# Linear attention with a gated feed-forward: batch 0's k and v in 96 partitions, Newton steps in PSUM, half exchanges as reductions, a new order

## The chip, the cores and the metric

The kernel runs on one core of a Trainium2 chip. The metric is the device time of one execution in microseconds. The core has a matrix engine (TensorE, PE in the profile, with its weight loads as PEld), VectorE (DVE), ScalarE (ACT), GpSimd (POOL) and SyncE (SP), which here issues every DMA. Each engine works through its own queue in order; engines wait for each other by semaphores.

## The reference

Two stages follow each other. Attention is linear, over 8 batches, 8 heads, 576 positions and 64 dimensions:

```python
q_s = exp(q - max(q, axis=-1));  q_s = q_s / (sum(q_s, axis=-1) + 1e-9)
k_s = exp(k - max(k, axis=2));   k_s = k_s / (sum(k_s, axis=2) + 1e-9)
kv  = einsum('bhsd,bhse->bhde', k_s, v)
out = einsum('bhsd,bhde->bhse', q_s, kv)
```

Its 4608 x 512 result x goes through a gated feed-forward with d_ff = 1536:

```python
xn = x / sqrt(mean(x * x, axis=-1) + 1e-6) * rms_g
g = xn @ w_gate;  val = xn @ w_val
return (g * sigmoid(g) * val) @ w_out
```

The weights arrive as 64-bit floats and are converted to 32 bits on the chip.

## The kernel before, in words

**Tiling.** Tokens are taken in 9 blocks (j) of 512, and d_ff in 12 chunks (i) of 128, so that the feed-forward has 108 steps s = 12 j + i. A step is `f1.s.0` and `f1.s.1` (gate and value products, L825, twelve matmuls each), `g_mul`, `silu`, `h_mul`, and `f2.s` (output product, L861). To keep 32-bit accuracy each operand is split into a high and a low part, and three products are summed: `w_hi` and `w_lo` split the gate and value weights, `o_hi` and `o_lo` the output weights, `h_hi` and `h_lo` the activations, `x_hi` and `x_lo` the input. `f2.0` to `f2.8` use plain 32-bit matmuls instead.

**Attention.** Batches b go by pairs of heads (g = 0 to 3). For k: `k_load`, `k_max` over a partition's positions (L445), `k_tr` and `k_top` (maximum over partitions), `k_diag` and `k_rows` (spread of the maximum to all rows), `k_sub` (L471), `k_exp`, then `k_mm` (L484) with v, whose extra column of ones yields the sum. 576 positions lie in 116 partitions of 5: 115 full ones and a last row that holds one position, loaded by a DMA of its own (for k, that position in all five places). In batch 0, v has no column of ones, and `k_mm` multiplies by `ones` in matmuls of their own (L490). Tiles of batch 0 for which no buffers are left lie in weight tiles not yet in use (`scratch`). From block 2 on q is held as 32 x 32 squares, with half of a head's dimensions in each group of 32 partitions, so that maxima and sums are exchanged between halves by `other_half` (L630), called by `q_half` and `q_half2`.

**Normalization.** `n_sum` sums squares by a matmul of mean weights into PSUM, `n_t` transposes, `n_y0` and `n_y1` compute 1/sqrt by a shift, a guess and three Newton steps on tiles of 128 x 16 in SBUF (L748 to L767), `n_rows` and `n_cols` spread the result. `g_mul` needs `n_rows` of its block.

**Weights.** `load_w.i.a` loads (a: gate, value, output); `conv_mul`, `conv_low`, `conv_shift`, `conv_sign` and `conv_add` turn 64 into 32 bits on ACT, DVE and POOL. All of it falls into block 0's time.

**Order.** A list of step names (`ORDER`) fixes the order in which instructions are issued, and so each engine's and SP's queue. A suffix `:A`, `:D` or `:P` puts a step on ACT, DVE or POOL. `warm` issues filler matmuls whose results nobody reads. PSUM has 8 banks: 2 for `ps_gv` (gate, value and `warm`), 4 for `ps_o`, 2 for `ps_a` (attention and `n_sum`). A tile pool hands out its buffers in turn, and the next user of a buffer waits for the last reader.

## Time and profile before

| | |
|---|---|
| median of 3 runs | 1056.67 us (1056.58 to 1057.47) |
| the profiled execution | 1055.17 us |
| its span, first to last instruction | 1053.4 us |
| mean granted TensorE clock | 0.986 |
| DMA | 57.62 MB, mean 55 GB/s |

A view of the profile gives busy time by engine; in the view by stage each row has start and end of the stage, its length, then for PE, PEld, DVE, ACT and POOL the busy time with the count of instructions, then the granted clock, the share of the 16 DMA engines that was busy, and GB/s. A row of a group has line, engine, operation, tiles (out<-in) and shapes, count, then busy us and mean ns, then the engine's idle time ahead of it and what ended it. A row of the timeline has start and duration, and in brackets the idle time ahead. Rows of waits give the waiting and the awaited instruction, total us, count and the longest.

### The profile page before, as it was taken

How to read it: one execution, taken by the hardware profiler on the slowest of the kernel's cores; microseconds unless marked ns; L12 is line 12 of the kernel's file. 1: busy time of each engine (PE TensorE's matmuls, PEld its weight loads, DVE VectorE, ACT ScalarE, POOL GpSimd, SP SyncE). 2: the span in 40 equal slices, each digit the busy share in tenths (PEclk: the TensorE clock that was granted, in tenths of full speed). 3: DMA queues.
4: the chain of work that ended last, by engine and by line, in shares of the span. 5: the costliest groups of instructions: out<-in, count | busy, mean ns of one | idle time of the engine just before them, and what ended most of it. 6: DMA issues, size and time to landing. Idle time of an engine off the chain costs nothing.

```text
span 1053.4 us, 14281 instructions
## 1 busy us (share of the span) xinstructions
PE 1015.6 (96%) x4972; PEld 809.4 (77%) x4972; DVE 603.8 (57%) x1180; ACT 573.6 (54%) x795; POOL 723.6 (69%) x623
## 2 busy tenths in 40 slices
...
GB/s 151 263 192 174 139 115 23 83 33 27 45 46 38 40 41 42 45 33 41 25 74 33 33 34 63 43 33 34 52 41 19 6 40 1 1 1 41 0 1 40
DMA packets 124884, 57.62 MB, mean 55 GB/s; under 512 B 95924, under 2 KB 118796, under 8 KB 124812
## 3 DMA queue, kind: packets, MB, share of 16 engines
...
q8 instruction: 39, 0.64, 0.3%
q14 instruction: 33, 0.27, 0.1%
...
## 4 chain that ended last, share of the span: by engine, by line
PE 59%; DVE 15%; DMA 12%; issue 4%; POOL 4%; ACT 4%; SPq 2%; ACTq 0%; DVEq 0%; POOLq 0%
PE ps_gv L825 35%; PE ps_o L861 20%; DMA kt<-in_k_dram 8%; DVE sw L630 4%; PE ps_a L688 2%; DVE cm L445 2%; DVE ke L471 1%; DVE gs L837 1%; SPq L558 1%; DVE w L382 1%; DMA raw<-in_moe_w_out_dram 1%; DVE kv_lo L532 1%; DVE gs L830 1%; DMA w<-in_k_dram 1%; POOL wl L802 1%
## 5 line engine op out<-in xcount | busy, mean ns | idle before, releaser
L802 POOL TENSOR_TENSOR wl<-w,wh 128x512 fp32r<-128x512 f32 x216 | 281.3, 1308 | 91.5 <-ACT wh L327 87.3
L825 PE MATMUL ps_gv<-xh,wh 128*128 128x512 f32 x864 | 244.0, 403 | 9.4 <-DVE gs L830 7.7
L825 PE MATMUL ps_gv<-xl,wh 128*128 128x512 f32 x864 | 233.8, 391 | 0.0
L825 PE MATMUL ps_gv<-xh,wl 128*128 128x512 f32 x864 | 233.5, 391 | 0.0
L825 PEld LDWEIGHTS ps_gv<-xh,wh 128*128 128x128 f32 x864 | 157.5, 189 | 44.4 <-issue 9.4
L825 PEld LDWEIGHTS ps_gv<-xl,wh 128*128 128x128 f32 x864 | 162.7, 188 | 35.6
L825 PEld LDWEIGHTS ps_gv<-xh,wl 128*128 128x128 f32 x864 | 162.7, 188 | 35.2
L846 POOL TENSOR_TENSOR hl<-gs,hh 128x512 fp32r<-128x512 f32 x99 | 128.2, 1295 | 67.7 <-ACT hh L327 64.8
L834 ACT ACTIVATE gs<-gs 128x512 f32<-128x512 f32 x108 | 68.2, 632 | 193.7 <-DVE gs L830 193.2
L830 DVE TENSOR_TENSOR gs<-ps_gv,r 128x512 f32<-128x512 f32 x108 | 74.4, 689 | 153.1 <-PE ps_gv L825 119.0
L810 POOL TENSOR_TENSOR ol<-w,oh 128x512 fp32r<-128x512 f32 x99 | 128.0, 1293 | 4.5 <-ACT oh L327 4.1
L837 DVE TENSOR_TENSOR gs<-ps_gv,gs 128x512 f32<-128x512 f32 x108 | 74.4, 689 | 95.8 <-PE ps_gv L825 76.5
L327 ACT CAST wh<-w 128x1024 fp32r<-128x1024 f32 x102 | 106.6, 1045 | 35.7 <-PE ps_gv L825 27.3
L861 PE MATMUL ps_o<-oh,hh 128*128 128x512 f32 x396 | 107.4, 393 | 0.0
L861 PE MATMUL ps_o<-ol,hh 128*128 128x512 f32 x396 | 106.9, 392 | 0.0
L861 PE MATMUL ps_o<-oh,hl 128*128 128x512 f32 x396 | 106.7, 392 | 0.0
L327 ACT CAST oh<-w 128x512 fp32r<-128x512 f32 x99 | 61.2, 618 | 62.6 <-PE ps_o L861 61.7
L327 ACT CAST hh<-gs 128x512 fp32r<-128x512 f32 x97 | 60.1, 619 | 64.0 <-DVE gs L837 61.1
L861 PEld LDWEIGHTS ps_o<-oh,hl 128*128 128x128 f32 x396 | 74.9, 189 | 15.8
L861 PEld LDWEIGHTS ps_o<-ol,hh 128*128 128x128 f32 x396 | 74.8, 189 | 16.0
L861 PEld LDWEIGHTS ps_o<-oh,hh 128*128 128x128 f32 x396 | 73.4, 188 | 14.9
L445 DVE TENSOR_REDUCE cm<-kt 116x128 f32<-116x640 f32 x30 | 39.0, 1301 | 62.4 <-DMA kt<-in_k_dram 62.3
...
## 6 DMA issues: line engine op xcount, KB each, us to landing
...
```

The source lines that it names most:

```text
L327: (e.copy if e is nc.scalar else e.tensor_copy)(dst, src)
L445: nc.vector.tensor_reduce(out=cm, in_=kt_[b, g].rearrange("p h j d -> p h d j"), axis=AX.X, op=ALU.max)
L630: nc.vector.tensor_copy(sw[32 * (a ^ 1):32 * (a ^ 1) + 32], st[32 * a:32 * a + 32])
L688: nc.tensor.matmul(px[:, c0:c1], lhsT=wt, rhs=mv[:, c0:c1], start=(i == 0), stop=(i == 2))
L802: on(nc.gpsimd).tensor_tensor(out=wl[:, a], in0=W(s % NF, a), in1=wh[:, a].bitcast(F32), op=ALU.subtract)
L810: on(nc.vector).tensor_tensor(out=ol, in0=W(s % NF, 2), in1=wo_[s][0].bitcast(F32), op=ALU.subtract)
L825: nc.tensor.matmul(pd[s], lhsT=m[:, a, c * P:(c + 1) * P], rhs=X[j, c][x], start=(n == 1), stop=(n == 3 * NKT))
L830: nc.vector.tensor_tensor(out=gs, in0=g_[s], in1=r_[s // NF], op=ALU.mult)
L834: nc.scalar.activation(g_[s], g_[s], AF.Silu)
L837: nc.vector.tensor_tensor(out=g_[s], in0=v_[s], in1=g_[s], op=ALU.mult)
L846: on(nc.gpsimd).tensor_tensor(out=hl, in0=g_[s], in1=h_[s][0].bitcast(F32), op=ALU.subtract)
L861: nc.tensor.matmul(po[t], lhsT=a[:, t * P:(t + 1) * P], rhs=w, start=(i == 0 and n == 0), stop=(i == NF - 1 and n == len(terms) - 1))
```

## The change

Batch 0's positions lie in 96 partitions of 6 (`C0`, `P0`), which leaves no last row, so that each k load is one DMA and each v load one per head; v gets its column of ones by `v_ones`, and `k_mm` is 12 matmuls without those by `ones`. The tiles of all four pairs lie in weight tiles. `k_max0` takes batch 0's maximum in three `tensor_tensor` steps. `k_sub` and `k_exp` of every batch write over k's own tile, and the tile `ke` is gone. `k_diag` may run on ACT, and does in all but one place. `other_half` and `n_cols` copy by a `tensor_reduce` over an axis of length one. The Newton steps keep `ms` and `u` in the PSUM bank that `n_sum` wrote, and each step multiplies in another sequence. In the last step, `f2` goes by token tile and then by term. Of `ORDER`, all lines are new; parts of it are shown. The first `warm` is 16 matmuls instead of 28; the other 20 calls of `warm`, two matmuls each, all stand ahead of `f1.1.0`, where before five of them stood between steps 9 and 10 and one later.

```diff
-constants k_load.0.0 q_load0.0.0 kv_zero0.0 warm.28 kv_zero0.1 k_load.0.1 kv_zero.4 kv_zero.5 kv_zero.6 k_load.0.2
...
-k_rows.0.0 k_max.0.2 warm.2.5 warm.2.1 v_load.0.3 k_sub.0.0 k_tr.0.2 warm.2.10 g_load q_max0.0.1 k_exp.0.0 load_w.0.0
-q_sum0.0.0 q_sub0.0.1:P load_w.1.0 k_top.0.1 load_w.2.0 k_max.0.3 load_w.3.0 q_exp.0.1 k_mm.0.0 k_load.1.0 k_diag.0.1
-q_max0.0.2 k_rows.0.1 load_w.0.1 k_tr.0.3 q_eps0.0.0 warm.2.2 k_top.0.2 q_sub0.0.2:P load_w.0.2 q_rec0.0.0 warm.2.6
-k_sub.0.1 load_w.1.1 warm.2.15 load_w.1.2 q_mul0.0.0:P q_exp.0.2 q_max0.0.3 q_load0.1.0 k_exp.0.1 q_sum0.0.1
...
-conv_low.0.2.1 w_lo.0.1:P warm.2.12 q_max0.1.0 conv_mul.2.0.2:A f1.0.0.0 k_top.1.0 conv_add.1.0.2:P f1.0.1.0
-conv_low.2.0.2 f1.0.0.1 conv_mul.1.2.1:A f1.0.1.1 conv_low.1.2.1 n_y0.0 f1.0.0.2 w_hi.1.0.2:A f1.0.1.2
-conv_shift.0.2.1 f1.0.0.3 conv_mul.3.0.2:A n_y1.0 f1.0.1.3 conv_low.3.0.2 w_lo.1.0:P n_rows.0 k_max.1.1
-conv_mul.2.2.1:A w_lo.1.1:P conv_low.2.2.1 g_mul.0 q_sub0.1.0:P conv_mul.3.2.1:A q_max0.1.1 conv_low.3.2.1 f1.1.0
...
-n_hi.5:A g_mul.59 n_lo.5:P silu.59 n_sum.5 h_mul.59 w_hi.61.0.2:A f2.58 n_t.5 h_hi.59:A w_lo.61.0:P q_max.7.0
...
+constants k_load.0.0 q_load0.0.0 v_ones.0.0 warm.16 k_load.0.1 v_ones.0.1 kv_zero0.0 q_load0.0.1 v_ones.0.2 v_ones.0.3
+kv_zero0.1 k_load.0.2 kv_zero.4 q_load0.0.2 kv_zero.5 kv_zero.6 kv_zero.7 v_load.0.0 kv_zero.0 kv_zero.1 k_load.0.3
+kv_zero.2 q_load0.0.3 kv_zero.3 v_load.0.1 k_max0.0.0 v_load.0.2 q_max0.0.0 k_tr.0.0 warm.2.0 v_load.0.3 k_top.0.0
+q_sub0.0.0:P k_diag.0.0:A k_rows.0.0 g_load k_sub.0.0 warm.2.1 q_exp.0.0 load_w.0.0 load_w.1.0 k_max0.0.1 k_load.1.0
+q_max0.0.1 k_tr.0.1 k_exp.0.0 warm.2.5 load_w.2.0 q_sum0.0.0 q_sub0.0.1:P load_w.3.0 k_top.0.1 k_load.1.1 k_mm.0.0
+q_max0.0.2 k_diag.0.1:A q_exp.0.1 k_max0.0.2 k_rows.0.1 warm.2.2 q_eps0.0.0 warm.2.6 k_max0.0.3 load_w.0.1 k_tr.0.2
+warm.2.10 load_w.0.2 q_rec0.0.0 q_sub0.0.2:P k_top.0.2 k_tr.0.3 warm.2.15 k_sub.0.1 k_diag.0.2:A k_rows.0.2
+q_mul0.0.0:P load_w.1.1 q_exp.0.2 warm.2.11 q_max0.0.3 load_w.1.2 k_exp.0.1 q_sum0.0.1 q_sub0.0.3:P q_t0.0.0
+q_load0.1.0 k_top.0.3 k_sub.0.2 k_diag.0.3:A q_exp.0.3 warm.2.3 k_eps.0.0 k_rows.0.3 q_c0.0.0:A q_eps0.0.1 k_mm.0.1
...
+k_tr.1.0 warm.2.8 conv_shift.0.2.1 conv_mul.1.0.2:A warm.2.12 w_lo.0.0:P n_y0.0 warm.2.13 k_top.1.0 warm.2.17
+conv_low.1.0.2 n_y1.0 warm.2.9 w_lo.0.1:P f1.0.0.0 conv_low.0.2.1 warm.2.18 k_diag.1.0:A conv_shift.1.0.2
+conv_mul.1.2.1:A f1.0.0.1 n_rows.0 conv_mul.2.0.2:A f1.0.1.0 conv_sign.1.0.2 f1.0.0.2 conv_low.2.0.2 f1.0.1.1
+conv_sign.0.2.1 conv_low.1.2.1 f1.0.0.3 conv_add.1.0.2:D conv_mul.2.2.1:A f1.0.1.2 conv_low.2.2.1 g_mul.0
+conv_add.0.2.1:P k_rows.1.0 w_hi.1.0.2:A f1.0.1.3 q_max0.1.0 warm.2.14 conv_shift.2.0.2 silu.0 load_w.4.0 warm.2.19
+w_lo.1.0:P k_sub.1.0 load_w.4.1 f1.1.0 load_w.4.2 q_max0.1.1 w_lo.1.1:P k_exp.1.0 n_cols.0 h_mul.0 q_sub0.1.0:P
...
+w_hi.59.0.2:A q_t.6.1 q_sum.6.3 h_lo.57:P f1.58.0 n_hi.5:A q_half2.6.3 o_hi.58:A w_lo.59.0:P q_load.7.0 n_lo.5:P
+f1.58.1 g_mul.58 silu.58 w_lo.59.1:P o_lo.58:P f2.57 h_mul.58 w_hi.60.0.2:A q_sum2.6.3 q_rec.6.3 h_hi.58:A w_lo.60.0:P
+q_max.7.0 h_lo.58:P f1.59.0 q_half.7.0 o_hi.59:A w_lo.60.1:P o_lo.59:P f1.59.1 g_mul.59 q_mul.6.3:P silu.59 q_max2.7.0
+q_sub.7.0:P n_sum.5 h_mul.59 w_hi.61.0.2:A f2.58 n_t.5 h_hi.59:A w_lo.61.0:P n_y0.5 q_hi.6.0:A q_hi.6.1:A n_y1.5
...
     SF = FULL * CH
+    C0 = 6
+    P0 = S // C0
+
+    def scratch0(wi, g):
+        return scratch(wi, g * 2 * C0 * D, [P0, 2, C0, D])
 
...
         hs = slice(2 * g, 2 * g + 2)
-        if b == 0 and g >= 2:
-            kt = scratch(3, (g - 2) * 640, [KP, 2, CH, D]).rearrange("p (h j d) -> p h j d", h=2, j=CH)
-        else:
-            kt = ap.tile([KP, 2, CH, D], F32, name="kt")
+        if b == 0:
+            kt_[b, g] = scratch0(3, g).rearrange("p (h j d) -> p h j d", h=2, j=C0)
+            nc.sync.dma_start(kt_[b, g], k[b, hs].rearrange("h (p j) d -> p h j d", j=C0))
+            return
+        kt = ap.tile([KP, 2, CH, D], F32, name="kt")
         nc.sync.dma_start(kt[:FULL], k[b, hs, :SF].rearrange("h (p j) d -> p h j d", j=CH))
...
         if (b, g) not in vt_:
-            if b == 0 and g >= 2:
-                vt_[b, g] = scratch(2, (g - 2) * 650, [KP, 2, CH, D]).rearrange("p (h j d) -> p j h d", j=CH, h=2)
-            elif b == 0:
-                vt = ap.tile([KP, CH, 2, D + 1], F32, name="vt").rearrange("p j h d -> p (j h d)")
-                vt_[b, g] = vt[:, :2 * CH * D].rearrange("p (h j d) -> p j h d", j=CH, h=2)
+            if b == 0:
+                n = 2 * C0 * (D + 1)
+                vt = scratch(2, g * n, [P0, n]) if g < 3 else scratch(1, 0, [P0, n])
+                vt_[b, g] = vt.rearrange("p (j h d) -> p j h d", j=C0, h=2)
             else:
...
         if b == 0:
-            nc.sync.dma_start(vt[:FULL].rearrange("p j h d -> p h j d"),
-                              v[b, hs, :SF].rearrange("h (p j) d -> p h j d", j=CH))
-        else:
             for h in range(2):
-                nc.sync.dma_start(
-                    vt[:FULL, :, h, :D],
-                    v[b, 2 * g + h, :SF].rearrange("(p j) d -> p j d", j=CH))
+                nc.sync.dma_start(vt[:, :, h, :D], v[b, 2 * g + h].rearrange("(p j) d -> p j d", j=C0))
+            return
+        for h in range(2):
+            nc.sync.dma_start(
+                vt[:FULL, :, h, :D],
+                v[b, 2 * g + h, :SF].rearrange("(p j) d -> p j d", j=CH))
         nc.sync.dma_start(
...
     def k_max(b, g):
-        cm = ap.tile([P, P], F32, name="cm")[:KP].rearrange("p (h d) -> p h d", h=2)
+        cm = ap.tile([P, P], F32, name="cm")[:KP if b else P0].rearrange("p (h d) -> p h d", h=2)
         nc.vector.tensor_reduce(out=cm, in_=kt_[b, g].rearrange("p h j d -> p h d j"), axis=AX.X, op=ALU.max)
...
 
+    def k_max0(b, g):
+        e = nc.vector
+        kt = kt_[b, g]
+        m = scratch(1, 2 * C0 * (D + 1) + g * C0 * D, [P0, 2, C0 // 2, D]).rearrange("p (h j d) -> p h j d", h=2, j=C0 // 2)
+        cm = cm_[b, g] = ap.tile([P, P], F32, name="cm")[:P0].rearrange("p (h d) -> p h d", h=2)
+        e.tensor_tensor(out=m, in0=kt[:, :, :C0 // 2], in1=kt[:, :, C0 // 2:], op=ALU.max)
+        e.tensor_tensor(out=m[:, :, 0], in0=m[:, :, 0], in1=m[:, :, 1], op=ALU.max)
+        e.tensor_tensor(out=cm, in0=m[:, :, 0], in1=m[:, :, 2], op=ALU.max)
+
     def k_tr(b, g):
         kps[b, g] = attn_ps(b == 0)
-        nc.tensor.transpose(out=kps[b, g][:, :KP], in_=cm_[b, g].rearrange("p h d -> p (h d)"),
-                            identity=ident[:KP, :KP])
+        n = KP if b else P0
+        nc.tensor.transpose(out=kps[b, g][:, :n], in_=cm_[b, g].rearrange("p h d -> p (h d)"),
+                            identity=ident[:n, :n])
 
...
         kx_[b, g] = small.tile([P, 1], F32, name="kx")
-        nc.vector.tensor_reduce(out=kx_[b, g], in_=kps[b, g][:, :KP], axis=AX.X, op=ALU.max)
+        nc.vector.tensor_reduce(out=kx_[b, g], in_=kps[b, g][:, :KP if b else P0], axis=AX.X, op=ALU.max)
 
...
         kd_[b, g] = ap.tile([P, P], F32, name="cm")
-        on(nc.vector).tensor_scalar_mul(kd_[b, g], ident, kx_[b, g])
+        scaled(kd_[b, g], ident, kx_[b, g], nc.vector)
 
     def k_rows(b, g):
-        mb = kps[b, g][:KP, P:2 * P]
-        nc.tensor.matmul(mb, lhsT=ones[:, :KP], rhs=kd_[b, g], start=True, stop=True)
+        n = KP if b else P0
+        mb = kps[b, g][:n, P:2 * P]
+        nc.tensor.matmul(mb, lhsT=ones[:, :n], rhs=kd_[b, g], start=True, stop=True)
         mb_[b, g] = mb.rearrange("p (h d) -> p h d", h=2)
...
     def k_sub(b, g):
-        if b == 0 and g >= 2:
-            ke = scratch(2, 1300 + (g - 2) * 640, [KP, CH, 2, D]).rearrange("p (j h d) -> p j h d", h=2, j=CH)
-        else:
-            ke = ap.tile([KP, CH, 2, D], F32, name="ke")
-        on(nc.vector).tensor_tensor(out=ke.rearrange("p j h d -> p h j d"), in0=kt_[b, g],
-                                in1=mb_[b, g].unsqueeze(2).broadcast_to([KP, 2, CH, D]), op=ALU.subtract)
-        ke_[b, g] = ke
+        n, c = (KP, CH) if b else (P0, C0)
+        ke = ke_[b, g] = kt_[b, g]
+        on(nc.vector).tensor_tensor(out=ke, in0=ke, in1=mb_[b, g].unsqueeze(2).broadcast_to([n, 2, c, D]),
+                                    op=ALU.subtract)
 
...
         ps = attn_ps(b == 0)
-        for j in range(CH):
-            n = KP if j == 0 else FULL
+        rows = [KP] + [FULL] * (CH - 1) if b else [P0] * C0
+        for j, n in enumerate(rows):
             for h in range(2):
-                nc.tensor.matmul(ps[h * D:(h + 1) * D, :D + (b > 0)], lhsT=ke[:n, j, h], rhs=vt[:n, j, h],
-                                 start=(j == 0), stop=(j == CH - 1))
-        if b == 0:
-            for j in range(CH):
-                n = KP if j == 0 else FULL
-                for h in range(2):
-                    nc.tensor.matmul(ps[h * D:(h + 1) * D, D:D + 1], lhsT=ke[:n, j, h], rhs=ones[:n, :1],
-                                     start=(j == 0), stop=(j == CH - 1))
+                nc.tensor.matmul(ps[h * D:(h + 1) * D, :D + 1], lhsT=ke[:n, h, j], rhs=vt[:n, j, h],
+                                 start=(j == 0), stop=(j == len(rows) - 1))
         kps[b, g] = ps
...
     def q_load0(j, g):
-        if j == 0 and g >= 2:
-            qt = scratch(3, 1280 + (g - 2) * TB, [P, TB])
+        if j == 0 and g == 3:
+            qt = ap.tile([P, TB], F32, name="r")
         else:
...
         for a in range(4):
-            nc.vector.tensor_copy(sw[32 * (a ^ 1):32 * (a ^ 1) + 32], st[32 * a:32 * a + 32])
+            nc.vector.tensor_reduce(out=sw[32 * (a ^ 1):32 * (a ^ 1) + 32], in_=st[32 * a:32 * a + 32].unsqueeze(2),
+                                    axis=AX.X, op=ALU.max)
         return sw
...
         if j == 0 and g < 3:
-            sq = fp.tile([P, TB], F32, name="gs", bufs=3) if g else scratch(3, 1280 + 2 * TB, [P, TB])
+            sq = fp.tile([P, TB], F32, name="gs", bufs=3)
         elif j and g == 0:
...
 
-    def n_eps(j):
-        ms_[j] = small.tile([P, M], F32, name="ms", bufs=1)
+    def n_y0(j):
+        ps = ms_[j]
+        ms_[j], u_[j] = ps[:, :M], ps[:, M:2 * M]
+        n_y[j] = small.tile([P, M], F32, name="y", bufs=2)
         nc.vector.tensor_scalar_add(ms_[j], dg_[j][:, :, 0], EPS_RMS)
-
-    def n_half(j):
-        u_[j] = small.tile([P, M], F32, name="u", bufs=1)
         nc.vector.tensor_scalar(out=u_[j].bitcast(I32), in0=ms_[j].bitcast(I32), scalar1=1, scalar2=None,
                                 op0=ALU.logical_shift_right)
-
-    def n_guess(j):
-        n_y[j] = small.tile([P, M], F32, name="y", bufs=2)
         nc.vector.tensor_scalar(out=n_y[j].bitcast(I32), in0=u_[j].bitcast(I32), scalar1=-1.0,
...
 
-    def n_newton(j, k):
+    def n_y1(j):
         y, u = n_y[j], u_[j]
-        if k % 3 == 0:
-            nc.vector.tensor_tensor(out=u, in0=y, in1=y, op=ALU.mult)
-        elif k % 3 == 1:
-            nc.vector.scalar_tensor_tensor(out=u, in0=u, scalar=-0.5, in1=ms_[j], op0=ALU.mult, op1=ALU.mult)
-        else:
+        for _ in range(3):
+            nc.vector.scalar_tensor_tensor(out=u, in0=y, scalar=-0.5, in1=ms_[j], op0=ALU.mult, op1=ALU.mult)
+            nc.vector.tensor_tensor(out=u, in0=u, in1=y, op=ALU.mult)
             nc.vector.scalar_tensor_tensor(out=y, in0=u, scalar=1.5, in1=y, op0=ALU.add, op1=ALU.mult)
...
             p = slice(32 * a, 32 * a + 32)
-            nc.vector.tensor_copy(yt[p], n_y[j][p].rearrange("p (t a) -> p a t", a=4)[:, a])
+            nc.vector.tensor_reduce(out=yt[p], in_=n_y[j][p].rearrange("p (t a) -> p a t", a=4)[:, a].unsqueeze(2),
+                                    axis=AX.X, op=ALU.max)
         y_[j] = yt
-
-    def n_y0(j):
-        for f in (n_eps, n_half, n_guess):
-            f(j)
-        for k in range(3):
-            n_newton(j, k)
-
-    def n_y1(j):
-        for k in range(3, 9):
-            n_newton(j, k)
 
...
             terms = ((hh, oh), (hh, ol), (hl, oh))
-        for n, (a, w) in enumerate(terms):
-            for t in range(T):
+        order = [(n, t) for n in range(len(terms)) for t in range(T)]
+        if s == NS - 1:
+            order.sort(key=lambda x: (x[1], x[0]))
+        for n, t in order:
+                a, w = terms[n]
                 nc.tensor.matmul(po[t], lhsT=a[:, t * P:(t + 1) * P], rhs=w, start=(i == 0 and n == 0),
```

480 lines of the change are left out of this document (236 added, 244 removed).

## The prediction

> **What bounds the kernel now.** I read the busy shares first, then the view of busy time by stage, then the timelines of the stages in which TensorE is not at its pace. All times are of the profiled execution.
>
> ```profile
> PE 1015.6 (96%) x4972; PEld 809.4 (77%) x4972; DVE 603.8 (57%) x1180; ACT 573.6 (54%) x795; POOL 723.6 (69%) x623
> ```
>
> TensorE is the engine to follow, but its 96% contains filler matmuls (`warm`), and a head in which no matmul of the feed-forward can start. By stage, cut at the first gate matmul (47.12), at later chunks' and blocks' starts and at the last matmul's end:
>
> ```profile
> core 0: us, PE busy (x) PEld busy (x) DVE busy (x) ACT busy (x) POOL busy (x), PEclk, DMA share, GB/s
> 47.12:58.20 11.08, 5.67 (x25) 4.35 (x25) 10.70 (x19) 9.74 (x13) 6.92 (x6) 0.96 0.37 113
> 58.20:66.50 8.30, 8.30 (x24) 6.62 (x25) 5.65 (x9) 4.44 (x6) 2.69 (x2) 0.64 0.68 184
> 66.50:141.50 75.00, 73.05 (x321) 48.57 (x320) 68.06 (x99) 54.39 (x70) 52.88 (x38) 1.00 0.62 183
> 141.50:175.74 34.24, 33.26 (x149) 23.59 (x150) 26.72 (x33) 21.61 (x32) 29.70 (x24) 1.00 0.15 37
> 175.74:294.23 118.49, 109.09 (x542) 87.77 (x540) 79.51 (x177) 65.52 (x90) 86.31 (x75) 0.99 0.19 43
> 294.23:848.00 553.77, 547.56 (x2772) 445.19 (x2773) 338.05 (x709) 316.53 (x435) 402.34 (x342) 1.00 0.16 39
> 848.00:1048.10 200.10, 200.07 (x883) 165.28 (x881) 49.73 (x86) 77.98 (x113) 125.08 (x100) 1.00 0.03 11
> ```
>
> A stage's length less its PE time is PE's idle time: 5.4, 0, 2.0, 1.0, 9.4, 6.2 and nothing, 24.0 in all. From 294 on, where most of the time lies, only 6.2 us can be had, and the matmuls of these stages stay as they are. What is left to gain lies in the 47.12 us ahead of the first gate matmul, in its wait, in the half clock behind it (8.30 at 0.64 loses about 3.0) and in the stages up to 294.
>
> What holds the head is the loading:
>
> ```profile
> 12.00:14.00 2.00, 1.89 (x9) 1.32 (x10) 1.78 (x3) 0.00 (x0) 0.00 (x0) 1.00 0.33 120
> 34.00:48.00 14.00, 14.00 (x61) 8.56 (x60) 8.64 (x16) 11.67 (x21) 6.46 (x7) 0.78 0.96 299
> 56.00:58.00 2.00, 0.00 (x0) 0.00 (x0) 2.00 (x4) 1.07 (x1) 0.00 (x0) 0.82 0.38 86
> 5.00:47.12 42.12, 35.24 (x255) 25.33 (x254) 24.93 (x54) 21.73 (x38) 13.41 (x13) 0.80 0.76 229
> 18.19 0.27 SPq L429 DMA_DIRECT2D w<-in_v_dram  x1
> 38.84 0.67 ACT L332 ACTIVATE w<-raw 128x512 f32<-128x512 f32 x1 [0.21 <-DMA raw<-in_moe_w_val_dram]
> 47.12 0.39 PE L825 MATMUL ps_gv<-xh,wh 128*128 128x512 f32 x1
> 58.20 2.04 PE L825 MATMUL ps_gv<-xh,wh 128*128 128x512 f32 x4 [5.41 <-DVE gs L830]
> ```
>
> From 12 to 14, where k and v in 115 partitions are what is under way, the DMA share is 0.33: 5.3 of 16 engines, 120 GB/s. Weights, in 128 partitions, get 0.96 and 299 GB/s. The last v of batch 0 is issued at 18.19 and the weights queue behind it; ACT begins on chunk 0's value weights only as they land, at 38.84, and 8.3 us later the first gate matmul runs.
>
> **Part 1, the loads: -8.9 us.** Batch 0's k and v are 8 x 0.295 = 2.36 MB, at 120 GB/s 19.7 us. What 96 partitions get is not in this trace. Lower bound: no more engines, and v, now in pieces of 64 elements as later batches' v is, at the 86 GB/s of 56 to 58, where such v is loading: 9.8 + 13.7 = 23.5, 3.8 longer. Upper bound: all engines, 16/5 of these rates but no more than the weights' 299: k 3.9, v at 275 GB/s 4.3, so 8.2, 11.5 shorter. I take 11.3, near the upper end, because the nearest row of a partition count that divides evenly is the 128-partition one. Eight transfers of k's and v's last row go, four issues come (v by head). Against it, `k_load.1.1` (0.29 MB in 115 partitions, 2.4 us) now stands ahead of `load_w.0.1`: 11.3 - 2.4 = 8.9. ACT's step moves to 30, the first gate matmul to 38. DVE's work must keep up: 24.93 us from 5 on, which ends by 30 if never idle, so 38 leaves 8 us for latencies. The other head edits cost or save little there:
>
> ```profile
> L445 DVE TENSOR_REDUCE cm<-kt 116x128 f32<-116x640 f32 x30 | 39.0, 1301 | 62.4 <-DMA kt<-in_k_dram 62.3
> L830 DVE TENSOR_TENSOR gs<-ps_gv,r 128x512 f32<-128x512 f32 x108 | 74.4, 689 | 153.1 <-PE ps_gv L825 119.0 <-PE ps_a L450 23.8 <-POOL wl L802 4.8
> L637 DVE TENSOR_TENSOR st<-st,sw 128x16 f32<-128x16 f32 x28 | 4.7, 169 | 0.6
> 7.79 1.04 POOL L582 TENSOR_TENSOR qt<-qt,st 128x512 f32<-128x512 f32 x1 [2.92 <-DVE st L578]
> ```
>
> By L637 and L830 an element costs DVE 1.05 ns over a fixed 0.15: `k_max0`'s 384, 128 and 128 elements take 1.1 us against 1.30. The 20 matmuls with `ones` go from a PE that waits there. Should POOL's passes (1.04 each) hold `k_max0`'s three instructions, up to 3 us come onto the first pair: 1031, to which I give 10%, inside the forecast's span.
>
> The Trainium skill, "DMA: Bandwidth & Descriptors", section "Why a DMA increments its semaphore by 16 and not by 1", says that a transfer runs on the largest number of engines up to 16 that divides its slowest dimension. By it 115 rows get 5 and 96 rows 16; the 5.3 above agree for 115, and no run here shows 96. "SBUF — State Buffer", section "Who interferes with whom", of the Trainium skill says that a DVE instruction with two SBUF inputs is held by a GpSimd instruction that reads SBUF, and a reduction never: that speaks against `k_max0`, and would be the 1031.
>
> **Part 2, Newton in PSUM: -3.5 us, and -2 of the half clock.**
>
> ```profile
> 47.57 0.50 DVE L748 TENSOR_SCALAR ms<-sq 128x16 f32<-128x16 f32 x1
> 48.00 2.45 POOL L387 TENSOR_TENSOR w<-w,raw 128x1024 int32<-128x1024 int32 x1
> 48.10 2.38 DVE L752 TENSOR_SCALAR u<-ms 128x16 int32<-128x16 int32 x1
> 55.63 0.71 DVE L771 STREAM_TRANSPOSE r<-y 128x512 f32<-128x512 f32 x1
> L763 DVE TENSOR_TENSOR u<-y 128x16 f32<-128x16 f32 x27 | 12.5, 463 | 0.9
> ```
>
> A shift of 16 elements takes 2.38 us and ends with POOL's addition, which began 0.1 us before it: DVE was held, not working. The mean of 463 ns against 169 (L637) for the same shape says that this is common. The twelve steps and one conversion (0.4) fill 47.57 to 55.63; at 0.2 a step they take 2.4 instead of 7.6, 5.2 saved. The new order puts more conversion ahead of `g_mul.0` (two `conv_sign` and a `conv_add` on DVE, against one `k_max`), which takes back some 1.7. The wait of 5.41 falls to about 2; of the 3.0 lost to the clock I take 2, as `warm.2.14` and `warm.2.19` now fill the gap. Should PSUM operands be held too, both terms are nothing; all steps at 0.17 and no conversion ahead would give 5.4 and 3.0.
>
> **Part 3, half exchanges, `k_diag`, order up to 294: -11 us.**
>
> ```profile
> L630 DVE COPY sw<-st 32x16 f32<-32x16 f32 x112 | 50.3, 449 | 2.0
> L630 DVE COPY sw<-sm 32x16 f32<-32x16 f32 x112 | 40.2, 359 | 2.0
> L455 DVE TENSOR_REDUCE kx<-ps_a 128x1 f32<-128x116 f32 x28 | 7.5, 270 | 8.1 <-PE ps_a L450 8.1
> L459 DVE TENSOR_SCALAR cm<-ident,kx 128x128 f32<-128x128 f32 x32 | 19.3, 604 | 0.7
> L327 ACT CAST kv_hi<-ot 128x128 fp32r<-128x128 f32 x4 | 1.2, 296 | 0.0
> 153.01 3.89 PE L392 MATMUL ps_gv<-mean_w 128*128 128x512 f32 x10 [0.54 <-DVE gs L830]
> 236.30 0.45 PE L688 MATMUL ps_a<-qh,kv_hi 128*128 128x384 f32 x1 [2.94 <-DVE kv_hi L334]
> 237.54 4.33 PE ps_o L861 x12
> 247.36 2.72 PE ps_o L861 x12
> ```
>
> Copies of 32x16 cost DVE 90.5 us. A reduction over one element has no row: 0.17 as the shape's other work, or 0.27 as the 128x116 reduction, so 224 of them cost 38 to 60 and 30 to 52 go; `k_diag` takes another 19.3 from DVE and gives ACT about 32 x 0.3. DVE sets no time where PE is full, so this counts only beside idle PE. From 66.5 to 175.7 that is 2.9 of idle time and 3.9 of filler at 153, which the new order no longer has: I take 4 of 6.8. From 175.7 to 294 it is 9.4, among it 2.94 for a `kv_hi` on DVE, and 1.6 behind it as twelve matmuls take 4.33 instead of 2.72; `kv_hi.2.1` goes to ACT. I take 7 of 11.
>
> **Part 4, from 294 on: -3.5 us of 6.2.** `n_sum` now stands two weight chunks behind `n_lo`, on which it waits once a block:
>
> ```profile
> PE ps_a L738 <- POOL ql L724: 4.7, 6, 1.6
> SPq L408 <- DVE ke L471: 184.5, 22, 14.0
> 1048.11 0.47 ACT L873 ACTIVATE gs<-ps_o,yt 128x256 f32<-128x256 f32 x1
> ```
>
> Five of these six lie here, 3.1 us. **k in place** frees k's buffer after its matmuls instead of after the subtraction. SP now waits 184.5 us in 22 loads for the subtraction, in future for PE, some us later, and DVE waits 62.3 / 30 = 2.1 us a load (L445) with `g_mul` and `h_mul` queued behind `k_max`, and PE's next PSUM buffer behind these. The order moves `k_max` back too; I cost it at nothing, the cover being the matmuls that PE has queued meanwhile (2.72 a dozen). The last chunk's products one token tile at a time save nothing: the chain to the end runs over `store.8.3` (at 1048.11), second on ACT, and its tile ends last in either order.
>
> **Sum.** -8.9 - 3.5 - 2 - 4 - 7 - 3.5 = -28.9. The profiled execution took 1055.17, 1.5 below the median of the runs: 1026.3 for it, 1028 for the median.
>
> **Rivals.** *Conversion becomes the bound* (17%): while weights are converted DVE is busy 68.06 of 75.00 us. If it cannot keep chunks 1 to 11 ahead of a PE that starts earlier, the 14.4 us of parts 1 and 2 are lost again by 150, and 2 of part 3's: -12.5, 1044. Against it: those 68 us contain stalls that go. *The loads do not spread* (6%): 3.8 + 2.4 longer to chunk 0, the other parts -20: -13.8, 1043. *All waits go* (15%): the first gate matmul at 34 (-13), 22 of the 24.0, and 8 of filler and clock: -43, 1014. *Slower* (6%): the later load of k holds `k_max`, and it `g_mul` and `h_mul`. It decides from 28.9 / 22 = 1.3 us of PE time a load; at 2 us, +44 - 28.9: 1072. For it: DVE waits there already. Against it: in five blocks full of such waits PE idles 6.2 us, and SP's 184.5 do no harm.
>
> **How the numbers follow.** The forecast, 1020 to 1036, holds 53%; no change, a mild case of the fourth rival, 3%. The range, 1012 to 1045, takes in the first three rivals and both ends of the DMA rate; outside it lie the slower case and the tails of the first and third. Under 0.2% (2 us) a difference can't be told from none. Faster 0.91, same 0.03, slower 0.06.
>
> **What would show it.** Part 1: a DMA share of 0.7 or more before 14, and the first gate matmul near 38; wrong if the share stays at 0.33. Part 2: Newton steps of 0.2 us and a gap of about 2 us before chunk 1. Part 3: exchanges of 0.17 to 0.27 us, block 1's first matmul near 153 instead of 175.7. Part 4: blocks of 108 to 109 us. The forecast falls if PE waits for conversions in the first block, or each block for `g_mul` behind `k_max`.

## The result, and the profile after

The changed kernel takes 1014.63 us in the median of 4 runs (1012.98 to 1016.58), against 1056.71 for the kernel before, measured beside it: a ratio of 0.9601, 95% interval 0.9583 to 0.9619. The profiled execution took 1016.58, its span 1014.8, the mean granted clock was 0.992. Forecast were 1028 and a range of 1012 to 1045: the sign and the range were right, the gain was larger than the sum said (38.6 us between the profiled executions, 28.9 forecast). Every later run had the kernel before measured beside it too, at medians of 1055.78 to 1057.08, so times of different runs can be compared to about 1 us.

The view of busy time by stage of the kernel after, cut at the same points (first gate matmul, chunk 1, block 1, block 2, block 7, last matmul's end), with the columns as before:

```profile
core 0: us, PE busy (x) PEld busy (x) DVE busy (x) ACT busy (x) POOL busy (x), PEclk, DMA share, GB/s
5.00:42.72 37.72, 30.48 (x185) 20.33 (x184) 26.56 (x69) 25.71 (x46) 14.03 (x15) 0.82 1.05 256
42.72:50.40 7.68, 7.49 (x33) 5.59 (x32) 6.41 (x8) 5.73 (x8) 5.22 (x4) 1.00 0.52 148
50.40:161.70 111.30, 109.19 (x483) 75.09 (x484) 91.42 (x144) 81.49 (x111) 80.99 (x59) 1.00 0.50 147
161.70:269.70 108.00, 107.81 (x551) 88.39 (x551) 69.93 (x180) 70.35 (x98) 92.97 (x82) 1.00 0.21 47
269.70:807.10 537.40, 537.40 (x2752) 441.16 (x2752) 270.31 (x673) 344.51 (x473) 396.76 (x338) 1.00 0.17 40
807.10:1009.10 202.00, 201.97 (x891) 166.74 (x889) 43.35 (x82) 79.20 (x114) 127.63 (x102) 1.00 0.03 12
```

And the stages of the kernel before that the prediction cut elsewhere, so that they can be laid beside these:

```profile
58.20:175.74 117.54, 114.61 (x493) 78.78 (x494) 100.43 (x139) 80.44 (x106) 85.26 (x63) 0.97 0.49 140
175.74:297.30 121.56, 112.16 (x555) 90.32 (x554) 82.11 (x181) 67.23 (x93) 89.25 (x78) 0.99 0.19 42
297.30:846.10 548.80, 542.59 (x2752) 441.06 (x2751) 333.59 (x704) 314.19 (x430) 397.50 (x339) 1.00 0.16 39
846.10:1048.10 202.00, 201.97 (x891) 166.87 (x889) 51.59 (x87) 78.60 (x114) 126.98 (x101) 1.00 0.03 11
```

| stage | before | after | difference | forecast |
|---|---|---|---|---|
| up to the first gate matmul | 47.12 | 42.72 | -4.4 | -8.9 |
| chunk 0 to chunk 1 | 11.08 | 7.68 | -3.4 | -3.5 |
| chunk 1 to block 1 | 117.54 | 111.30 | -6.2 | -2 and -4 |
| block 1 | 121.56 | 108.00 | -13.6 | -7 |
| blocks 2 to 6 | 548.80 | 537.40 | -11.4 | -3.5 |
| blocks 7 and 8 | 202.00 | 202.00 | 0 | 0 |
| last matmul to the end of the span | 5.3 | 5.7 | +0.4 | 0 |
| sum | 1053.4 | 1014.8 | -38.6 | -28.9 |

**The row that settles most is that of blocks 2 to 6.** The count of matmul records is the same, 2752, so the two rows compare like with like. Before, 548.80 less 542.59 is 6.2 us of idle time, and after it is none. But the stage became 11.4 us shorter: the other 5.2 came out of *busy* time. The groups of matmuls that waited say where. First before, then after; a group has count, busy us, mean ns, and the idle time ahead of it:

```profile
L688 PE MATMUL ps_a<-qh,kv_lo 128*128 128x256 f32 x24 | 7.5, 312 | 1.5 <-DVE kv_lo L532 1.4
L688 PE MATMUL ps_a<-qh,kv_hi 128*128 128x256 f32 x24 | 7.4, 308 | 1.8 <-ACT kv_hi L332 1.5
L738 PE MATMUL ps_a<-ql,mean_w 128*128 128x512 f32 x5 | 2.4, 479 | 2.7 <-POOL ql L724 2.7
```

```profile
L697 PE MATMUL ps_a<-qh,kv_hi 128*128 128x256 f32 x24 | 6.8, 282 | 0.0
L697 PE MATMUL ps_a<-qh,kv_lo 128*128 128x256 f32 x24 | 6.8, 281 | 0.0
L747 PE MATMUL ps_a<-ql,mean_w 128*128 128x512 f32 x5 | 1.9, 387 | 0.0
```

The matmul that waits no longer overlaps with the ones before it: a matmul of 512 columns lasts 0.39 us, but a dozen of them in a row take 2.72, which is 0.23 each. One that starts alone counts as busy for its whole 0.39. Each wait therefore costs its idle time and, beside it, the lost overlap, which the trace books as work. The means above show only part of this. If each matmul of the trace is counted by the time that it adds to TensorE's busy time (from the latest end so far to its own end), the 80 products of `qh` with `kv_hi` and `kv_lo` in blocks 2 to 6, of all shapes, add 15.2 us before and 11.1 after, and the ten of `n_sum` 3.5 and 2.3. That is 5.3 us, all that went; the 40 products of `ql`, which never waited, add 5.6 in both.

VectorE and the steps that the change touched, from the groups of the kernel after:

```profile
L638 DVE TENSOR_REDUCE sw<-sm 32x16 f32<-32x16 f32 x112 | 18.0, 161 | 2.1
L638 DVE TENSOR_REDUCE sw<-st 32x16 f32<-32x16 f32 x112 | 18.0, 161 | 2.1
L769 DVE TENSOR_TENSOR ps_a<-ps_a,y 128x16 f32<-128x16 f32 x27 | 4.9, 182 | 0.9
L664 DVE SCALAR_TENSOR_TENSOR sm<-sm,sw 128x16 f32<-128x16 f32 x28 | 13.0, 466 | 0.2
```

The exchanges cost VectorE 36.0 us instead of 90.5, a Newton multiplication 182 ns instead of 463, and the mean of the nine shifts is 182 ns where one had lasted 2.38 us. Part of it comes back behind the exchanges: the two steps that combine the halves, with two inputs in SBUF each, have means of 406 (L646) and 466 ns (L664), where they had 169 and 177. The 25 of these 56 instructions that ran beside a GpSimd instruction had a mean of 769 ns, the 31 others 162 to 177. The 56 cost 24.4 us instead of 9.7, so VectorE gains some 40 us by the exchanges and not 54.

The head, by the stages of 4 us and the timelines of SP's queue, ScalarE, GpSimd and TensorE:

```profile
2.00:6.00 4.00, 4.00 (x13) 3.16 (x13) 1.78 (x4) 0.00 (x0) 3.04 (x20) 1.00 0.90 234
6.00:10.00 4.00, 2.37 (x12) 1.37 (x10) 0.60 (x2) 2.20 (x3) 1.04 (x1) 1.00 1.19 241
10.00:14.00 4.00, 2.30 (x22) 1.57 (x23) 3.93 (x9) 1.74 (x3) 1.30 (x2) 0.68 1.23 228
14.00:18.00 4.00, 4.00 (x23) 3.09 (x19) 3.48 (x10) 0.63 (x3) 2.02 (x2) 0.50 1.34 193
```

```profile
9.26 5.11 SPq L436 DMA_DIRECT2D w<-in_v_dram  x6
...
20.96 3.67 SPq L416 DMA_DIRECT2D kt<-in_k_dram  x1
24.68 0.41 SPq L363 DMA_DIRECT2D raw<-in_moe_w_val_dram  x1
...
33.62 0.66 ACT L332 ACTIVATE w<-raw 128x512 f32<-128x512 f32 x1 [2.79 <-DMA raw<-in_moe_w_val_dram]
35.95 2.08 PE L741 MATMUL ps_a<-sq,mean_w 128*128 128x512 f32 x2 [3.05 <-ACT sq L714]
38.05 2.72 POOL L796 TENSOR_TENSOR wl<-w,wh 128x512 fp32r<-128x512 f32 x2 [1.17 <-ACT wh L327]
38.75 4.13 PE L392 MATMUL ps_gv<-mean_w 128*128 128x512 f32 x10
42.72 0.40 PE L819 MATMUL ps_gv<-xh,wh 128*128 128x512 f32 x1
```

In 96 partitions the DMA engines are busy from the start (a share over 1 counts packets that overlap). From 2 to 18 us the share is 1.16 and the rate 224 GB/s; in the kernel before these 16 us had 0.49 and 155 GB/s, and the 0.33 and 120 of the prediction were their lowest stretch. By stages the rate is now 193 to 241 GB/s, not the 299 of the weights. The last v is issued before 14.4 instead of at 18.19; but `load_w.0.1` leaves only at 24.68, because SP was held for 3.67 us at the last-row load of `k_load.1.1`, which the new order put ahead of it. ScalarE gets chunk 0's value weights at 33.62 instead of 38.84, 5.2 earlier.

What follows is no longer loading. GpSimd has split chunk 0's gate weights at 39.3 and its value weights at 40.8 (the two of the row at 38.05), and yet the first gate matmul starts at 42.72, without idle time ahead of it. TensorE was busy with other work: it had waited 3.05 us for ScalarE's `sq`, its granted clock was 0.5 from 35.3 to 42.2, and largely at this clock the ten filler matmuls of `warm` that are queued ahead took 4.13 us.

### The profile page after: what moved, and what is told of

It reads as the page before. It is cut to its first block, busy times and chain, and to the rows that moved or that the text cites. A ratio compares the mean times of both kernels' runs of the same rounds, so it can differ in the third digit from the quotient of the medians.

```text
span 1014.8 us, 14207 instructions
## 1 busy us (share of the span) xinstructions
PE 997.7 (98%) x4896; PEld 800.0 (79%) x4896; DVE 509.3 (50%) x1153; ACT 608.6 (60%) x850; POOL 722.0 (71%) x625
## 4 chain that ended last, share of the span: by engine, by line
PE 86%; DMA 5%; SPq 3%; ACT 2%; POOL 1%; issue 1%; DVE 1%; ACTq 0%; DVEq 0%; POOLq 0%
PE ps_gv L819 53%; PE ps_o L858 27%; PE ps_a L697 2%; PE ps_a L498 2%; DMA vt<-in_v_dram 1%; DMA raw<-in_moe_w_out_dram 1%; DMA qt<-in_q_dram 1%; DMA w<-in_moe_w_val_dram 1%; DMA w<-in_moe_w_out_dram 1%; SPq L439 1%; SPq L363 1%; PE ps_a L480 1%; POOL wl L796 1%; SPq L416 1%; DMA kt<-in_k_dram 1%
## 5 line engine op out<-in xcount | busy, mean ns | idle before, releaser
L819 PE MATMUL ps_gv<-xh,wh 128*128 128x512 f32 x864 | 240.6, 399 | 1.2 <-ACT wh L327 1.0
L327 ACT CAST wh<-w 128x1024 fp32r<-128x1024 f32 x97 | 101.8, 1049 | 45.4 <-PE ps_gv L819 31.2
L327 ACT CAST hh<-gs 128x512 fp32r<-128x512 f32 x98 | 60.7, 619 | 38.0 <-DVE gs L831 37.1
```

The costliest lines, as they stand in the source:

```text
L327: (e.copy if e is nc.scalar else e.tensor_copy)(dst, src)
L819: nc.tensor.matmul(pd[s], lhsT=m[:, a, c * P:(c + 1) * P], rhs=X[j, c][x], start=(n == 1), stop=(n == 3 * NKT))
```

## The experiments

The theory after the result: VectorE's exchanges and Newton steps are held by GpSimd, and what stands behind them makes TensorE wait in every block, at a price above its idle time. The rivals: the new order alone takes the waits away; the k tile in place sets k's loads free; the layout is the larger part. The first kernels take single parts of the change back; the `b_` kernels put single parts into the kernel before.

**`a_copy`: the exchanges and column copies are copies again.**

```diff
-            nc.vector.tensor_reduce(out=sw[...], in_=st[...].unsqueeze(2), axis=AX.X, op=ALU.max)
+            nc.vector.tensor_copy(sw[...], st[...])
...
-            nc.vector.tensor_reduce(out=yt[p], in_=n_y[j][p].rearrange(...)[:, a].unsqueeze(2), axis=AX.X, op=ALU.max)
+            nc.vector.tensor_copy(yt[p], n_y[j][p].rearrange(...)[:, a])
```

> The changed kernel with the half exchanges and n_cols as copies again. Holding theory (DVE held by POOL in copies made PE wait before): PE idle time returns in blocks 1 to 6, +4 to +10 over 1014.6, so 1019 to 1025; the copies' mean goes from about 0.17 back to 0.36 or more. Order theory (the waits went because steps were moved): DVE busy grows by about 40 us but PE does not wait, within 2 of 1014.6.

Measured: 1046.37 us, ratio 0.9905 (0.9888 to 0.9922), 31.7 more than the kernel after. That is the holding theory's sign, but far above the 1019 to 1025 that were expected from it. Block 1 takes 118.4 us, the later ones 110.4 to 111.7. In its waits of TensorE and its groups of VectorE:

```profile
PE ps_a L480 <- ACT cm L332: 15.5, 14, 2.7
```

```profile
L638 DVE COPY sw<-st 32x16 f32<-32x16 f32 x112 | 82.1, 733 | 2.0
```

The timeline of the place of the longest of these waits shows the chain, an answer for each engine:

```profile
245.31 2.83 DVE L638 COPY sw<-sm 32x16 f32<-32x16 f32 x4
248.18 0.69 DVE L656 TENSOR_REDUCE sm<-qt 128x16 f32<-128x512 f32 x1
248.90 0.70 DVE L638 COPY sw<-sm 32x16 f32<-32x16 f32 x4
249.63 0.28 DVE L471 TENSOR_REDUCE kx<-ps_a 128x1 f32<-128x116 f32 x1
...
249.94 0.40 ACT L332 ACTIVATE cm<-ident,kx 128x128 f32<-128x128 f32 x1 [4.34 <-DVE kx L471]
...
245.21 1.30 POOL L794 TENSOR_TENSOR wl<-w,wh 128x512 fp32r<-128x512 f32 x1
246.46 1.29 POOL L802 TENSOR_TENSOR ol<-w,oh 128x512 fp32r<-128x512 f32 x1
251.08 1.05 POOL L670 TENSOR_TENSOR qt<-qt,sm 128x512 f32<-128x512 f32 x1 [3.32 <-DVE sm L667]
...
250.40 0.77 PE L480 MATMUL ps_a<-cm,ones 128*116 128x128 f32 x2 [2.70 <-ACT cm L332]
```

Four copies take 2.83 us while GpSimd works, to 247.75; the next four, with GpSimd idle, 0.70. `k_top` (L471) is queued behind them, ScalarE's `k_diag` behind `k_top`, and `k_rows` (L480) on TensorE behind that. This is how an exchange that TensorE never waits for costs TensorE time.

The whole trace says the same as this place. Of the 224 copies of the exchanges, the 93 with no GpSimd instruction at the same time took 161 to 171 ns each; the 131 others had a mean of 983 ns and up to 2.43 us. In the kernel after, 185 of the 224 reductions ran beside a GpSimd instruction, and all of these took 156 to 168 ns.

**`a_newton`: the Newton steps' two tiles stand in SBUF again.**

```diff
-        ps = ms_[j]
-        ms_[j], u_[j] = ps[:, :M], ps[:, M:2 * M]
+        ms_[j] = small.tile([P, M], F32, name="ms", bufs=1)
+        u_[j] = small.tile([P, M], F32, name="u", bufs=1)
```

> The changed kernel with ms and u of the Newton steps in SBUF again. Holding theory: steps of up to 1.2 or 2.4 us return, the gap before the second chunk grows by 2 to 5, and some block starts wait too: 1017 to 1021. Order theory: the later g_mul has slack, within 2 of 1014.6.

Measured: 1027.72 us, ratio 0.9732 (0.9709 to 0.9756), 13.1 more than after, where at most 1021 was expected. The stretch from chunk 0 to chunk 1 is 9.4 us, block 1 takes 114.2, the later ones 108.5 to 109.8; the steps last 722 and 678 ns on average, and `k_rows` waits 9.9 us in 7 places. So Part 2 isn't a matter of the head alone: eight more blocks have such steps. Here too the trace separates held from free: in the kernel before, the 60 of 108 steps with no GpSimd instruction beside them took 174 to 179 ns and the other 48 a mean of 1035; in the kernel after, 96 of the 108 ran beside GpSimd and took 169 to 195 ns. Steps on PSUM are not held.

**`a_held`: both of these, and every `k_diag` on VectorE; layout and order stay new.** The diff is those of `a_copy` and `a_newton`, and in the order `k_diag.b.g:A` becomes `k_diag.b.g`.

> The new order and batch 0's new layout, but copies, Newton in SBUF and k_diag on DVE as before. If the order and the loads are most of the gain: under 1022. If the freed DVE is: 1028 or more, with PE idle over 10 us after the first gate matmul.

Measured: 1081.65 us, ratio 1.0234 (1.0217 to 1.0252), slower than the kernel before; 1028 or more was expected if the freed VectorE is most of the gain. Block 1 and blocks 2 to 6, and the largest wait of TensorE:

```profile
166.70:291.21 124.51, 112.02 (x552) 90.75 (x550) 96.57 (x182) 66.97 (x93) 90.86 (x81) 0.96 0.18 41
291.21:872.43 581.22, 549.86 (x2752) 445.82 (x2750) 372.72 (x696) 335.81 (x456) 398.17 (x339) 0.99 0.16 37
```

```profile
PE ps_a L480 <- DVE cm L334: 40.2, 14, 6.2
```

The new order is no gain by itself. With the old instructions it costs 32 us in blocks 2 to 6 against the old order (581.22 against 548.80; k in place, which this kernel has too, isn't told apart from it). It presumes a VectorE that isn't held.

**`b_free`: the kernel before, its order and layout kept, with the exchanges as reductions, Newton in PSUM, and `k_diag` on ScalarE.**

```diff
-        on(nc.vector).tensor_scalar_mul(kd_[b, g], ident, kx_[b, g])
+        scaled(kd_[b, g], ident, kx_[b, g], nc.vector)
...
-            nc.vector.tensor_copy(sw[...], st[...])
+            nc.vector.tensor_reduce(out=sw[...], in_=st[...].unsqueeze(2), axis=AX.X, op=ALU.max)
...
-        ms_[j] = small.tile([P, M], F32, name="ms", bufs=1)
+        ps = ms_[j]
+        ms_[j], u_[j] = ps[:, :M], ps[:, M:2 * M]
```

> The kernel before, in its old order and old layout, with exchanges as reductions, Newton in PSUM and k_diag on ACT. If the freed DVE is most of the gain: 1035 or less. If order and loads are: 1043 to 1053, the gain being about the 3.5 us of the first wait and the 2.9 us of a kv_hi wait.

Measured: 1033.6 us, ratio 0.9785 (0.9767 to 0.9803), some 23 us, over half of the whole gain, and under the 1035 that was expected if the freed VectorE is most of it. Block 1 and blocks 2 to 6:

```profile
171.84:282.22 110.38, 109.47 (x556) 89.23 (x555) 62.61 (x176) 67.12 (x95) 89.49 (x79) 1.00 0.21 46
282.22:824.46 542.24, 539.20 (x2752) 440.91 (x2751) 267.56 (x684) 322.26 (x450) 396.71 (x339) 1.00 0.17 39
```

11.2 us go in block 1 and 6.6 in blocks 2 to 6, and here too busy time falls with the same 2752 matmuls (542.59 to 539.20). The wait for `ql` at `n_sum` stays, 3.3 us in 5 places. What `k_diag` on ScalarE adds to this no run tests alone.

**`b_reduce` and `b_newton`: of that, the reductions alone, and Newton in PSUM alone.**

> The kernel before with nothing changed but the half exchanges and the four column copies, which are reductions over an axis of length 1. If held copies are the larger part of what b_free gained (23.2 us): 1040 to 1046 us, blocks 2 to 6 near 108.5, and no wait of TensorE behind the exchange's followers. If the Newton steps are most of it: 1050 to 1056, blocks at 109 and more as before. In the changed kernel the copies put back cost 31.7 us; a cost that depends on the order would show as clearly less here.

> The kernel before with nothing changed but the Newton steps' two tiles, which stand in PSUM. If the parts simply add, this takes what b_reduce leaves of b_free's 23.2 us: 5 to 10 us, so 1047 to 1052, and the idle stretch from the first pooled matmul to chunk 1 falls from 11.1 to about 8.5. If the two cover one another (either alone leaves VectorE late): under 4 us, and b_reduce and this sum to much less than 23.2.

Measured: `b_reduce` 1039.54 us, ratio 0.9840 (0.9824 to 0.9857); `b_newton` 1043.50 us, ratio 0.9884 (0.9867 to 0.9902). The sum is 2.8%, that of `b_free`, which has `k_diag` on ScalarE besides, 2.15%: the two cover one another by some 0.6%, and neither is the whole. `b_newton` gained more than was expected of it (1047 to 1052), `b_reduce` just more (1040 to 1046). They work in the main at different places. Block 1 and blocks 2 to 6 of `b_reduce`:

```profile
175.36:287.98 112.62, 109.68 (x555) 89.18 (x554) 68.88 (x175) 66.34 (x91) 89.50 (x79) 1.00 0.20 45
287.98:831.22 543.24, 539.46 (x2752) 440.77 (x2750) 311.53 (x704) 315.41 (x430) 396.08 (x339) 1.00 0.17 39
```

Chunk 0 to chunk 1, the 8.30 us behind it, and blocks 2 to 6 of `b_newton`:

```profile
47.76:55.01 7.25, 5.60 (x26) 4.35 (x25) 6.87 (x19) 6.96 (x11) 6.08 (x6) 1.00 0.36 116
55.01:63.31 8.30, 7.94 (x29) 5.45 (x30) 7.93 (x13) 8.19 (x10) 3.82 (x4) 1.00 0.41 89
...
291.45:836.57 545.12, 540.57 (x2752) 441.01 (x2751) 296.91 (x704) 316.56 (x430) 397.55 (x339) 1.00 0.17 39
```

The reductions take 8.9 us from block 1 (121.56 to 112.62). Newton in PSUM takes 3.8 from the gap before chunk 1 (11.08 to 7.25), and with the gap goes the reduced clock behind it: 1.00 here, 0.64 in the kernel before. In `b_free`, with the same steps, the gap is 8.30 us with a wait of 2.53 in it, and the clock is 0.5 for 3.4 us behind it; why its wait is longer than the 1.65 of `b_newton` stays open. In the new order, with Newton in PSUM, the copies cost 31.7 us; in the old order they cost 16.2 with the old Newton steps, and 9.9 with those in PSUM (`b_newton` against `b_free`, `k_diag` included). So the cost of held copies depends on the order: 131 of the 224 lie beside a GpSimd instruction in `a_copy` and 68 in the kernel before, and other steps stand behind them.

**`a_rows95`: batch 0's k and v loads are cut into 95 rows and 1.**

```diff
-            nc.sync.dma_start(kt_[b, g], k[b, hs].rearrange("h (p j) d -> p h j d", j=C0))
+            for r in (slice(0, P0 - 1), slice(P0 - 1, P0)):
+                nc.sync.dma_start(kt_[b, g][r], k[b, hs].rearrange("h (p j) d -> p h j d", j=C0)[r])
...
-                nc.sync.dma_start(vt[:, :, h, :D], v[b, 2 * g + h].rearrange("(p j) d -> p j d", j=C0))
+                for r in (slice(0, P0 - 1), slice(P0 - 1, P0)):
+                    nc.sync.dma_start(vt[r, :, h, :D], v[b, 2 * g + h].rearrange("(p j) d -> p j d", j=C0)[r])
```

> The changed kernel with each of batch 0's k and v loads cut into 95 rows and 1 row, everything else the same. If 96 rows run on more engines than 95 or 115: the DMA share before 14 falls from about 1 to about 0.35, the last v lands some 10 us later, the first gate matmul moves from 42.7 to 47 or later: 1018 to 1026. If the number of rows does not matter: only twelve more issues of about 0.4 us, under 1016.

Measured: 1029.14 us, ratio 0.9746 (0.9728 to 0.9764), 14.5 more than after and 3 above the upper end of what was expected. The first gate matmul stands at 54.94, block 1 at 174.72, and the blocks are those of the kernel after to 0.2 us. The stage of 10 to 14 us:

```profile
10.00:14.00 4.00, 1.93 (x7) 1.06 (x7) 3.06 (x6) 1.68 (x3) 0.40 (x1) 0.88 0.35 104
```

A share of 0.35 is 5.6 of 16 engines, against 1.23 with 96 rows; the Trainium skill's rule in "DMA: Bandwidth & Descriptors", that a transfer runs on the largest number of engines up to 16 that divides its slowest dimension, gives 5 for 95 rows and 16 for 96, and agrees. The kernel also issues twice as many of these DMAs, so not all of the 14.5 us is the rate: SP was held for 14.03 us by twelve issues of v, from 16.63 on.

**`a_ke`: batches 1 to 7 get a tile `ke` of their own again.**

```diff
-        ke = ke_[b, g] = kt_[b, g]
+        kt = ke = kt_[b, g]
+        if b:
+            ke = ap.tile([KP, 2, CH, D], F32, name="ke")
+        ke_[b, g] = ke
```

> The changed kernel with a tile of its own for k's exponent in batches 1 to 7, so that k's buffer is free after the subtraction. If in-place costs nothing: within 1.5 of 1014.6. If the later load of k costs PE time: 1010 or less.

Measured: 1012.9 us, ratio 0.9592 (0.9571 to 0.9612), blocks of 106.9 to 107.9. It can't be told from the kernel after, though it lies 1.7 below it, just outside the 1.5 expected. In blocks 2 to 6, where the later load was feared, the two traces differ by 0.2 us (537.1 against 537.3 between the blocks' first matmuls), so k in place costs nothing there. From chunk 1 to block 1, `a_ke` takes 109.5 us against 111.3; whether that is k in place or scatter stays open.

**`a_nsum`: `n_sum.j` stands right behind `n_lo.j`.**

```diff
-q_half2.3.3 o_hi.22:A w_lo.23.0:P q_load.4.0 n_lo.2:P f1.22.1 g_mul.22 silu.22 w_lo.23.1:P o_lo.22:P f2.21 h_mul.22
+q_half2.3.3 o_hi.22:A w_lo.23.0:P q_load.4.0 n_lo.2:P n_sum.2 f1.22.1 g_mul.22 silu.22 w_lo.23.1:P o_lo.22:P f2.21
```

> The changed kernel with n_sum of blocks 1 to 8 moved back to stand right behind n_lo. If PE's wait for n_lo was a term of its own: the pitch of the two n_sum matmuls goes from 0.46 to 1.2 to 1.7 a block, +5 to +9 in all, 1020 to 1023. If POOL is early enough now: within 2.

Measured: 1020.01 us, ratio 0.9657 (0.9638 to 0.9675), 5.4 more than after, at the lower end of what was expected if that wait is a term of its own. Blocks 2 to 6:

```profile
266.71:809.12 542.41, 538.73 (x2751) 440.76 (x2750) 267.98 (x673) 345.12 (x473) 396.80 (x338) 1.00 0.17 39
```

5.0 us are lost there, 1.0 a block, of which 3.7 show as idle and 1.3 as busy time. This divides the 11.4 of these blocks along one path of kernels: 548.80 before, 542.24 with the freed VectorE (`b_free`), 542.41 with the rest of the change but `n_sum`'s place (`a_nsum`), 537.40 with that. The shares hold for this path alone: taken in the other order, the new order without the freed VectorE (`a_held`) loses 32.4 and the freed VectorE then gains 43.8.

**`a_loads`, `a_tail`, `a_best`: what more is to be had.** `a_loads` puts chunk 0's value and output weights (`load_w.0.1`, `load_w.0.2`) ahead of batch 1's k, `k_load.1.1` behind the weights of chunk 1, and `k_max.1.1` behind `g_mul.0`; `a_tail` moves `store.8.3`, which needs the last matmul's tile, behind `store.8.1` and `store.8.2`, so that these no longer queue behind it on ScalarE, and puts `store.8.1` on VectorE (the last store's second half ran there already); `a_best` has both, and a tile of its own for each half of the last store.

```diff
-f2.106 h_mul.107 h_hi.107:A h_lo.107:P f2.107 store.8.0:A store.8.3 store.8.1:A store.8.2:A
+f2.106 h_mul.107 h_hi.107:A h_lo.107:P f2.107 store.8.0:A store.8.1:D store.8.2:A store.8.3
```

> The changed kernel with chunk 0's value and output weights loaded ahead of k of batch 1, and k_max.1.1 behind g_mul.0. If the landing of load_w.0.1 (ACT waits for it until 33.6) sets the first gate matmul: that moves from 42.7 to 36 to 39, and the time to 1008 to 1012. If the attention chain sets it: under 1 us of change there.

> The changed kernel with the last store's second half on VectorE and the last two entries of the order exchanged, so that ScalarE's second half no longer waits for its tile behind the last matmul. If that wait sets the end: the stretch from TensorE's end to the span's end goes from 5.7 to about 4.6 us and the time to about 1013.5. If the last transfer sets it: 5.7 us stays and the time is that of the changed kernel. The blocks stay at 107 to 108 us and chunk 1 to block 1 at 111.

> The changed kernel with the head's loads as in a_loads, the end as in a_tail, and the last store's halves in tiles of their own. If the head's gain (1.7 us) and the end's (about 1.1 us) are both real and add: 1010 to 1011.5 us. If the head's is only the scatter of the DMA: 1012.5 to 1014.5, with the first pooled matmul anywhere from 38 to 42 us.

Measured: `a_loads` 1012.93 us, ratio 0.9589 (0.9573 to 0.9606); `a_tail` 1013.56, ratio 0.9599 (0.9581 to 0.9617); `a_best` 1011.78, ratio 0.9587 (0.9566 to 0.9608). All three intervals hold the 0.9601 of the kernel after, so no gain is established by the times; `a_best` lies between what was expected with both gains and with the end's alone. The traces show one at the end: in `a_tail` the span ends 4.0 us behind the last matmul instead of 5.7, which is 1.7 less where 1.1 was expected. In the head they show what sets the first gate matmul. The table has the four kernels whose head is that of the kernel after, and the two with moved loads, by the time in us:

| kernel | TensorE's wait for `sq` | then the clock is 0.5 for | ten fillers take | first gate matmul | block 1 |
|---|---|---|---|---|---|
| after | 3.05 | 6.8 | 4.13 | 42.7 | 161.7 |
| `a_tail` | 2.91 | 3.4 | 2.63 | 41.1 | 159.9 |
| `a_ke` | 2.60 | 3.4 | 3.50 | 40.9 | 158.1 |
| `a_nsum` | 2.07 | 0 | 2.56 | 39.2 | 157.7 |
| `a_loads` | 0.33 | 0 | 2.54 | 37.7 | 157.6 |
| `a_best` | 0.33 | 0 | 2.57 | 37.1 | 157.5 |

Where the loads are not moved, ScalarE waits 1.8 to 2.8 us for the value weights, with the `sq` that TensorE needs queued behind, and the reduced clock turns this 1 us of scatter into 3.5 at the first gate matmul. The moved loads take both away: ScalarE's wait is 0.02 us. Against `a_nsum`, which had no reduced clock, they gain 1.6 to 2.2 us at the first gate matmul and nothing at block 1. Their worth is thus the reduced clock that they avoid, up to some 4 us of an execution. The runs of `a_loads` lie within 0.9 us of each other, but those of `a_best`, with the same loads, within 5.3, so what it is worth on average stays open.

## Why the prediction was right, and where it was too small

**Part 1 (-8.9, measured -4.4) was mis-sized.** The mechanism is shown by `a_rows95`: with 95 rows the head is 12 us longer. The term of 11.3 for the loads was more than twice too large: the weights' first load is issued at 15.24 instead of 20.28, 5.0 earlier. Both of its rates were off. The start was taken at 120 GB/s, from the 2 us in which the DMA engines were least busy; the 16 us from 2 on had 155. And v was assumed at 275 GB/s, where the stages in which it loads show 193 to 228. By 155 and 224 GB/s the 2.36 MB take 15.2 and 10.5 us, an estimate of 4.7 less. `k_load.1.1` ahead of `load_w.0.1` was priced at 2.4 us by bytes; its last-row DMA alone held SP for 3.67. What came on top is the clock, which the prediction did not count in the changed head: with it at 0.5 the first gate matmul stood at 42.7, without it at 39.2 (`a_nsum`), 7.9 earlier than before. That this lies near the 8.9 is luck, since the loads gained 5.

**Part 2 was right in the place that it priced**: -3.4 against -3.5 for the gap; steps of 0.18 us where 0.2 was forecast; and the clock at 1.00, where 2 of the 3 us lost were to come back. The idle time in the gap went to 0.2 us and not to 2, as fillers of `warm` run in it. `b_newton` shows that the steps alone can bring the gap and the clock, without the new order's fillers, though `b_free` keeps 3.4 us of reduced clock with the same steps. The prediction's doubt, that PSUM operands are held too, is settled by the 96 steps beside GpSimd at 169 to 195 ns. It left out that the eight later blocks have such steps too: `b_newton` takes another 3.7 us from blocks 2 to 6.

**Part 3 was right up to block 1 and failed behind it.** Chunk 1 to block 1: -6.2 against -2 and -4. There idle time fell by only 0.8 us (2.9 to 2.1); the rest is busy time, where the 3.9 us of filler and the reduced clock had been. For block 1 stood "I take 7 of 11", and it was 13.6: the 9.4 us of idle time went but for 0.2, and 4.4 of busy time with it (some 0.9 of that as four matmuls fewer), where the prediction had allowed 1.6. The exchanges' duration (0.161) came out below the lower bound of 0.17, and that the steps behind them would be held instead (406 and 466 ns) was not counted.

**Part 4 holds the step that failed.** It took 3.5 "of 6.2", because "from 294 on, where most of the time lies, only 6.2 us can be had, and the matmuls of these stages stay as they are". They did not: 2752 matmuls were busy for 5.2 us less. The mechanism, freed waits, was the one forecast; the size was bounded wrongly. The bound read from idle time was no bound, since a lone matmul behind a wait is longer in the trace than one in a row. The prediction had this effect in its own rows (twelve matmuls in 4.33 instead of 2.72) and used it at that one place.

The weight loads would have shown it. Their busy time in blocks 2 to 6 is the same before and after, 441.06 and 441.16 us, so it is a measure of the work: as a share of the stage it was 80% in blocks 2 to 6 and 74% in block 1 before, and 83% in blocks 7 and 8, where nothing waits. By this estimate 441.06 at 82.6% would take 534 us, 15 less than 548.80; 11.4 came. For block 1, 90.32 at 82.6% gives 109, 12 less; 13.6 came. The Trainium skill, "Perfetto Trace Analysis", section "Identifying the Most-Contended Engine", says that the busy share of matmuls is no good measure of how near TensorE is to its limit, and to judge its headroom by that of its weight loads and by the share of peak arithmetic. The trace agrees on the weight loads; the prediction read the wrong one of the two columns.

With the bound goes the sentence "DVE sets no time where PE is full, so this counts only beside idle PE": the freed VectorE gave 6.6 us in blocks 2 to 6 of the old order (`b_free`), where at most the 0.4 beyond `n_sum`'s waits was counted for it, and `n_sum`'s move gave 5.0 there (`a_nsum`), where five waits of 3.1 us were.

**What was costed at nothing** was nothing as far as shown: k in place in blocks 2 to 6 (`a_ke`), and the last chunk's order, as the last matmul's end and the end of the span lie 5.7 us apart instead of 5.3. No run takes that order back alone.

**The rivals.** *Conversion becomes the bound* fell: from chunk 1 to block 1 TensorE idles 2.1 of 111.3 us. *The loads do not spread* fell with the share of 0.9 and more. *Slower* through the later k load fell with `a_ke`. *All waits go* gave 1014 and lies nearest the time, in part by luck: of its 22 us of idle time 21.5 went, but it had the first gate matmul at 34, which stands at 42.7, and the lost overlap, which it didn't count, made up for that. The 1031 by a held `k_max0` isn't there: in the timeline one of its instructions was held for some 0.7 us beside GpSimd's pass,

```profile
13.74 1.29 POOL L590 TENSOR_TENSOR qt<-qt,st 128x512 f32<-128x512 f32 x1 [0.31 <-DVE st L586]
14.16 1.01 DVE L460 TENSOR_TENSOR w<-w 96x128 f32<-96x128 f32 x1
```

where the answer on its line gives shortest, median and longest of the four such instructions in ns:

```profile
L460 DVE TENSOR_TENSOR w<-w x4: 286/286/1014, 4.7 to 16.1; 96x128 f32<-96x128 f32 x4
```

The Trainium skill's rule that the prediction named ("SBUF — State Buffer", "Who interferes with whom": two SBUF inputs are held, a reduction never) agrees with this row, and with the exchanges: the reductions' mean was 161 ns, that of the copies, which by the same section may take the shared port too, up to 733. How a slower kernel could have come about, no rival had: `a_held` shows it, the new order without the freed VectorE.
